# Buffer pools first in SBUF, x on a second queue, one output store, and a last weight load cut into 104 and 24 rows

## Chip, cores and metric

The kernel runs on one core of one Trainium2 chip. The metric is the device time of the program in microseconds (us), and lower is better. A run is one execution; the executions of one kernel lie within a few tenths of a per cent of each other. Now and then a run is far slower than the others of its kernel. Such runs are left out of every comparison here; there was one, a run of e9 with 240.59 us, whose granted clock was 1.0 as in the others, and it is marked.

## The reference

One decode step for four sequences: attention over a window of cached keys and values, and beside it an MLP block, all added to the input.

```python
# B=4, D=576, 32 query heads, 16 key/value heads of 128; F=4608; bf16
W = 2048                                    # the last 2048 positions of the cache
xn = layernorm(x)
q  = xn @ wq                                # [4, 32, 128]
p  = softmax(q @ k[:, :, -W:].T * 128**-0.5)
A  = (p @ v[:, :, -W:]) @ wo
# B: xn plus gelu(layernorm(xn) @ w1) shifted by rows and @ w2, then gelu(layernorm(.) @ w3) @ w4
# with one position per sequence every shift leaves zeros, so w1 and w2 drop out
out = x + A + xn + gelu(layernorm(xn) @ w3) @ w4
```

Every byte of wq, the K and V windows, wo, w3 and w4 is used once: the profile counts 87.17 MB read from HBM. There is little arithmetic per byte.

## The kernel before

The kernel is written around the stream of loads. They all go through the queue that SyncE issues, in the order in which they are needed: x, wq, then K and V of the sixteen heads with wo and w3 between them, and w4 at the end. Each K or V load brings 128 rows of 16,384 bytes, one row to a partition. Seven buffers hold K and V; wq, w3 and w4 use one buffer in turn.

```python
const = tile_pool("const", bufs=1)      # SBUF pools, in the order in which they get addresses
small = tile_pool("small", bufs=2)
kvp   = tile_pool("kv", bufs=7)
ktp   = tile_pool("kt", bufs=3)
ptp   = tile_pool("pt", bufs=3)
wp    = tile_pool("w", bufs=1)
wop   = tile_pool("wo", bufs=2)

x_bf = const.tile([B, D], BF16)
nc.sync.dma_start(out=x_bf[:], in_=x2)
wq_main = A_wq[0:KJ * P, :].rearrange("(p j) n -> p j n", j=KJ)
for j in range(KJ):                                            # four loads with 8 KB rows
    nc.sync.dma_start(out=wq_sb[:, j * NQ:(j + 1) * NQ], in_=wq_main[:, j, :])
# [... the rest of wq ...]

def load_kv(kind, h):
    t = kvp.tile([P, NC, Dh], BF16, tag="kv")                  # 128 x 16,384 bytes
    nc.sync.dma_start(out=t[:].rearrange("p c d -> p (c d)"),
                      in_=win[:, h].rearrange("b (p c) d -> p b (c d)", c=NC))

W4_PIECES = [0, 9, 18, 27, 32, 36]                             # five pieces of w4, in blocks of 1,152 bytes a row
def load_w4():
    for lo, hi in zip(W4_PIECES, W4_PIECES[1:]):
        # [... src is the half of w4 that the piece lies in ...]
        nc.sync.dma_start(out=t[:, lo:hi, :], in_=src[:, lo - e * NFH:hi - e * NFH, :])

def acc_matmuls(lhsT, rhs):                                    # four rows in each quadrant of acc
    for i in range(NQD):
        nc.tensor.matmul(out=acc[i * QD:i * QD + B, :], lhsT=lhsT, rhs=rhs[:, i * CW:(i + 1) * CW], ...)

# [... attention and the first matmul of the MLP ...]
for lo, hi in pieces[2:]:                                      # the last pieces of w4, as they land
    mlp_out(lo, hi)
fin = const.tile([P, CW], out.dtype)
nc.vector.tensor_copy(out=fin[:], in_=acc[:])
for i in range(NQD):                                           # four stores of four rows
    eng = nc.sync if i % 2 == 0 else nc.scalar
    eng.dma_start(out=o2[:, i * CW:(i + 1) * CW], in_=fin[i * QD:i * QD + B, :])
```

## Time and profile before

| | before |
|---|---|
| time | 216.24 us, median of 2 runs (216.18 to 216.3) |
| span of the profiled run | 214.6 us |
| PE, DVE and ACT busy | 56%, 55%, 33% |
| a K or V packet of 16,384 bytes | 611 ns, the next one 607 ns later on the same engine |
| first packet of wq starts | 2.15 us |
| last piece of w4 lands, first and last of sixteen engines | 205.50 and 210.21 us |
| end of fin to end of the span | 3.30 us |

The packet times come from the packet records of the trace, the landings from its semaphore updates: a whole load has sixteen, which I read as one from each of the sixteen DMA engines when its share is done. All times are counted from the profile's zero. The recorded prediction and expectations count packets and landings from a moment 0.24 us earlier: their 2.39 and 210.45 are the profile's 2.15 and 210.21. A difference of two such times isn't touched, but where they measure from an instruction to a landing, the figure is 0.24 us too long.

The first view is the profile's page of the kernel before: the span, the busy time of each engine, and in 40 slices of the span the busy share of the sixteen DMA engines in tenths and the GB/s they moved; then two DMA queues with packets, MB and busy share.

```profile
span 214.6 us, 6449 instructions
PE 121.0 (56%) x2893; PEld 94.9 (44%) x2893; DVE 118.0 (55%) x223; ACT 70.1 (33%) x258; POOL 6.1 (3%) x14
...
DMA  5999999999999999999999999999999999999960
GB/s 207 429 437 434 428 429 425 425 425 437 426 429 423 437 431 419 439 425 434 431 428 425 428 428 430 422 434 431 429 418 428 437 419 425 437 427 422 419 262 12
...
q1 hardware_dynamic: 7080, 87.17, 95.7%
q8 instruction: 22, 0.36, 0.6%
```

No compute engine is busy for more than 56% of the span, and the DMA engines are at 90% or more in slices 2 to 38. The load stream bounds the kernel. Time can be lost or won only at its head, by its rate in the middle, or in the two slices at its end.

The end of the chain of waits of the kernel before says the same (columns: start, duration, what ran or was waited for).

```profile
182.78 27.43 DMA w_sb<-in_B_w_dram
210.21 0.04 issue
210.26 0.68 PE acc L247 x16
...
210.96 0.31 DVE fin L480
```

The last link is a wait for the load of w4; only 16 matmuls and one copy stand between it and the stores.

The timeline of the kernel before, at its two ends (start, duration, engine, line, operation, output and input, count; in brackets the idle time before and what ended it; "q" behind an engine's name is its issuing of DMAs):

```profile
0.73 0.36 SPq L87 DMA_DIRECT2D x_bf<-in_A_x_dram  x1
...
1.16 1.31 SPq L92 DMA_DIRECT2D wq_sb<-in_A_wq_dram  x3
...
207.14 0.73 PE L247 MATMUL acc<-w_sb,gT 128*4 128x144 bf16 x36 [1.17 <-DMA w_sb<-in_B_w_dram]
...
208.88 0.77 PE L247 MATMUL acc<-w_sb,gT 128*4 128x144 bf16 x20 [1.00 <-DMA w_sb<-in_B_w_dram]
...
210.26 0.65 PE L247 MATMUL acc<-w_sb,gT 128*4 128x144 bf16 x16 [0.61 <-DMA w_sb<-in_B_w_dram]
...
210.96 0.31 DVE L480 CAST fin<-acc 128x144 bf16<-128x144 f32 x1 [5.87 <-PE acc L247]
211.29 0.63 SPq L483 DMA_DIRECT2D out_dram<-fin  x2
211.30 0.92 ACTq L483 DMA_DIRECT2D out_dram<-fin  x2
```

At the head, x is issued before wq and holds it up by 0.43 us. At the end, PE waits for the third, fourth and fifth piece of w4 in turn.

The 22 packets of instruction fetch (q8, 16 KB and 935 ns each) fall on eight of the sixteen engines in turn, and each sets its engine back by more than 1 us. (The packet records name no engine; that the same eight serve in turn is read from the landings.) Before the first fetch, at 15.01 us, the sixteen landings of a load lie within 0.57 us; in the next load one comes 1.58 us after the first, and the fifteen others still lie within 0.58. In the last piece, with two or three fetches for each of the eight, six of the sixteen landings come within 0.26 us of the first, two after 1.05 and 1.82 (why these two are late isn't shown), three after 3.1 to 3.3, and five after 4.2 to 4.7.

### The profile page before, as it was taken

What the parts mean: (1) busy time and instruction counts of PE and PEld (TensorE: products, weight loads), DVE (VectorE), ACT (ScalarE), POOL (GpSimd) and SP (SyncE); (2) the same over time, 40 slices, a digit from 0 to 9 for tenths busy, and PEclk for the clock granted to TensorE, in tenths of its full rate; (3) what the DMA queues carried; (4) which work ended last, traced back from release to release, by engine and by line L of the source; (5) the groups of instructions that cost most, each with busy time, mean ns of one, the idle gap of its engine ahead of it and who ended that gap; (6) DMA issues with size and microseconds to landing.
All of it is one profiled execution on the core that took longest, in us unless ns stands there. A gap on an engine that the chain in (4) does not pass through costs nothing. (4 is left out here: it accounts for less than half of the span.)

```text
span 214.6 us, 6449 instructions
## 1 busy us (share of the span) xinstructions
PE 121.0 (56%) x2893; PEld 94.9 (44%) x2893; DVE 118.0 (55%) x223; ACT 70.1 (33%) x258; POOL 6.1 (3%) x14
## 2 busy tenths in 40 slices
PE   0461355647470017157999577677474705779752
PEld 0350143445360015145899456555453604557641
DVE  5608799766470047348610798785573924854210
ACT  0000005571634001607070045570725340709600
POOL 5400100000000000000000000000000000000000
PEclk9999999999999999999999999999999999999995
DMA  5999999999999999999999999999999999999960
GB/s 207 429 437 434 428 429 425 425 425 437 426 429 423 437 431 419 439 425 434 431 428 425 428 428 430 422 434 431 429 418 428 437 419 425 437 427 422 419 262 12
DMA packets 7123, 87.58 MB, mean 408 GB/s; under 512 B 820, under 2 KB 824, under 8 KB 1336
## 3 DMA queue, kind: packets, MB, share of 16 engines
q1 hardware_dynamic: 7080, 87.17, 95.7%
q8 instruction: 22, 0.36, 0.6%
q14 instruction: 5, 0.04, 0.0%
q10 hardware_dynamic: 16, 0.00, 0.0%
HBM read 87.17 MB, written 0.00 MB: 406 GB/s over the span
## 5 line engine op out<-in xcount | busy, mean ns | idle before, releaser
L302 ACT ACTIVATE pt<-S 32x128 bf16<-32x128 f32 x256 | 68.5, 268 | 92.0 <-issue 55.3
L259 DVE STREAM_TRANSPOSE kt<-kn 128x1024 int32<-128x1024 int32 x64 | 74.3, 1205 | 11.4 <-DMA kn<-in_A_k_cache_dram 11.4
L313 PE MATMUL O<-pt,vn 128*128 128x8 bf16 x1024 | 37.4, 169 | 43.2 <-DMA vn<-in_A_v_cache_dram 41.7
L313 PEld LDWEIGHTS <-vn 128*128 128x128 bf16 x1024 | 34.4, 105 | 51.3 <-DMA vn<-in_A_v_cache_dram 43.6
L273 PE MATMUL S<-qz,kt 128*128 128x32 bf16 x1024 | 39.1, 189 | 25.2 <-DVE kt L259 25.2
L273 PEld LDWEIGHTS <-kt 128*128 128x128 bf16 x1024 | 33.6, 106 | 36.1 <-DVE kt L259 30.4
L287 DVE TENSOR_REDUCE m<-mxT 8x1 f32<-8x128 f32 x16 | 4.4, 277 | 42.6 <-PE mxT L285 42.6
L316 PE MATMUL O<-pt,ones_bf 128*128 128x64 bf16 x128 | 17.1, 226 | 0.0
L302 ACT ACT_TABLE_LOAD x1 | 1.3, 1283 | 32.6 <-DVE mx L280 32.6
L368 PEld LDWEIGHTS <-w_sb 128*128 128x128 bf16 x144 | 11.4, 164 | 0.5 <-issue 0.4
L368 PE MATMUL AB<-ln2T,w_sb 128*128 128x4 bf16 x144 | 11.5, 202 | 0.0
L280 DVE TENSOR_REDUCE mx<-S 128x8 f32<-128x512 f32 x16 | 10.4, 652 | 1.0 <-PE S L273 1.0
L295 PE MATMUL S<-dg,ones_bf 8*128 8x512 bf16 x16 | 9.6, 601 | 0.1
L265 PE MATMUL S<-negbig,ohT 4*128 4x512 bf16 x16 | 9.6, 601 | 0.0
L316 PEld LDWEIGHTS <-ones_bf 128*128 128x128 bf16 x128 | 8.4, 104 | 0.0
L370 PE MATMUL AB<-ln2T,w_sb 128*128 128x4 bf16 x36 | 7.3, 202 | 0.0
L247 PE MATMUL acc<-w_sb,gT 128*4 128x144 bf16 x144 | 4.8, 294 | 2.8 <-DMA w_sb<-in_B_w_dram 2.8
L324 DVE TENSOR_REDUCE dn<-O 128x8 f32<-128x64 f32 x16 | 3.3, 208 | 5.5 <-PE O L316 5.5
L375 DVE COPY g_x<-AB 128x144 f32<-128x144 f32 x1 | 0.3, 307 | 10.7 <-PE AB L370 10.7
L285 PE MATMUL mxT<-ident_f,mx 128*8 128x128 f32 x16 | 6.0, 374 | 0.3 <-DVE mx L280 0.3
L370 PEld LDWEIGHTS <-w_sb 128*128 128x128 bf16 x36 | 5.9, 165 | 0.0
L247 PEld LDWEIGHTS <-gT 128*4 128x4 bf16 x144 | 3.4, 104 | 3.6 <-issue 3.5
(72 smaller groups left out, 64.9 us busy)
## 6 DMA issues: line engine op xcount, KB each, us to landing
kn<-in_A_k_cache_dram SPq DMA_DIRECT2D x16, 2048.0 KB, 29.3
vn<-in_A_v_cache_dram SPq DMA_DIRECT2D x16, 2048.0 KB, 27.0
wo_sb<-in_A_wo_dram SPq DMA_DIRECT2D x4, 1152.0 KB, 28.8
w_sb<-in_B_w_dram SPq DMA_DIRECT2D x2, 2304.0 KB, 31.8
wq_sb<-in_A_wq_dram SPq DMA_DIRECT2D x4, 1024.0 KB, 4.9
w_sb<-in_B_w_dram SPq DMA_DIRECT2D x3, 1296.0 KB, 32.8
w_sb<-in_B_w_dram SPq DMA_DIRECT2D x2, 576.0 KB, 32.2
w_sb<-in_B_w_dram SPq DMA_DIRECT2D x1, 720.0 KB
```

The lines of the kernel that those rows point to most:

```text
L247: nc.tensor.matmul(out=acc[i * QD:i * QD + B, :], lhsT=lhsT, rhs=rhs[:, i * CW:(i + 1) * CW], start=False, stop=False, skip_group_check=True)
L259: nc.vector.transpose(out=kt[:], in_=src)
L265: nc.tensor.matmul(out=S_ps[h][:].rearrange("p g k j -> p (g k) j"), lhsT=ohT[:], rhs=nb, start=True, stop=False, skip_group_check=True)
L273: nc.tensor.matmul(out=S_ps[h][:, s * (SC // NQD) + g].rearrange("p k j -> p (k j)"), lhsT=kt[:, ib, g * NQD:(g + 1) * NQD, e:2 * QD:2].re ...
L280: nc.vector.reduce_max(out=mx[:], in_=S_ps[h][:].rearrange("p g k j -> p j (g k)"), axis=AX.X)
L285: nc.tensor.transpose(out=mxT[:], in_=st[h][:], identity=ident_f[:])
L295: nc.tensor.matmul(out=S_ps[h][:].rearrange("p g k j -> p (g k) j"), lhsT=ones_bf[0:NJ, :], rhs=dg, start=False, stop=False, skip_group_ch ...
L302: nc.scalar.activation(out=PT[h][kb * QD:(kb + 1) * QD, :, c4, :], in_=S_ps[h][c4 * QD:(c4 + 1) * QD, :, kb, :], func=ACT.Exp, scale=scale)
L313: nc.tensor.matmul(out=O_ps[h][:, 0:NJ], lhsT=vn[:, g * NQD + s, :], rhs=pt[:, g, s, :], start=(g == 0 and s == 0), stop=False, skip_group ...
L316: nc.tensor.matmul(out=O_ps[h][:, NJ:].rearrange("p (c j) -> p c j", j=NJ), lhsT=ones_bf[:], rhs=pt[:, g:g + DG, s, :], start=False, stop= ...
L368: nc.tensor.matmul(out=g_ps[:, i, :], lhsT=w3[:, j * F + e * (F // 2) + f0:j * F + (e + 1) * (F // 2):NFH], rhs=ln2T[:, j, :], start=False ...
L370: nc.tensor.matmul(out=g_ps[:, i, :], lhsT=w3[:, KJ * F + f0:KJ * F + F // 2:NFH], rhs=ln2T[:, KJ + e, :], start=False, stop=False, skip_g ...
```

## The change

The intent: start the stream earlier (x from ScalarE's queue, wq in fewer and longer rows), relieve some of the engines at the end (the last piece of w4 as 104 rows and 24 rows), and store once instead of four times. For the single store all 128 rows of acc are written by matmuls with 32 columns, most of them zero. The pools of the load buffers now come first in SBUF. The sum of x and xn (xsum) takes the buffer of xn_f. The helper that transposes K only moves within the file.

```diff
-    const = ctx.enter_context(tc.tile_pool(name="const", bufs=1))
-    small = ctx.enter_context(tc.tile_pool(name="small", bufs=2))
     kvp = ctx.enter_context(tc.tile_pool(name="kv", bufs=NKV))
-    ktp, ptp, wp, wop                      [in this order]
+    wp, wop, ktp, ptp, const, small        [in this order]
 [...]
-    nc.sync.dma_start(out=x_bf[:], in_=x2)
-    wq_main = A_wq[0:KJ * P, :].rearrange("(p j) n -> p j n", j=KJ)
-    for j in range(KJ):
-        nc.sync.dma_start(out=wq_sb[:, j * NQ:(j + 1) * NQ], in_=wq_main[:, j, :])
+    nc.scalar.dma_start(out=x_bf[:], in_=x2)
+    wq_main = A_wq[0:KJ * P, :].rearrange("(p j) n -> p (j n)", j=KJ)
+    for e in range(2):
+        lo, hi = e * 2 * NQ, (e + 1) * 2 * NQ
+        nc.sync.dma_start(out=wq_sb[:, lo:hi], in_=wq_main[:, lo:hi])
 [...]
-            nc.sync.dma_start(out=t[:, lo:hi, :], in_=src[:, lo - e * NFH:hi - e * NFH, :])
+            for p0, p1 in ((0, P),) if hi < NF else ((0, 104), (104, P)):
+                nc.sync.dma_start(out=t[p0:p1, lo:hi, :], in_=src[p0:p1, lo - e * NFH:hi - e * NFH, :])
 [...]
-    gT = const.tile([P, NF, B], BF16)
+    gT = const.tile([P, NF, QD], BF16)     [op likewise, and idz for the first matmuls into acc]
+    nc.gpsimd.memset(gT[:], 0.0)
 [...]
-            nc.tensor.matmul(out=acc[i * QD:i * QD + B, :], lhsT=lhsT, rhs=rhs[:, i * CW:(i + 1) * CW],
+            nc.tensor.matmul(out=acc[i * QD:(i + 1) * QD, :], lhsT=lhsT, rhs=rhs[:, i * CW:(i + 1) * CW],
 [...]
-    for i in range(NQD):
-        eng = nc.sync if i % 2 == 0 else nc.scalar
-        eng.dma_start(out=o2[:, i * CW:(i + 1) * CW], in_=fin[i * QD:i * QD + B, :])
+    nc.sync.dma_start(out=o2.rearrange("b (i n) -> i b n", i=NQD), in_=fin[0:P:RS, :])
```

One effect isn't in the diff: in the built kernels the K and V buffers, and those of w, wo, kt and pt, start at multiples of 256 bytes within a partition before the change (the first K buffer at byte 38,144), and 128 bytes past one after it (at byte 16,512), because what stands ahead of them is now four small constants, 128 bytes in all, no longer the pools const and small.

More of the change, by code (lines that the diff above doesn't have):

```diff
@@ L71 @@
     ctx.enter_context(tc.manual_schedule())
+    kvp = ctx.enter_context(tc.tile_pool(name="kv", bufs=NKV))
+    wp = ctx.enter_context(tc.tile_pool(name="w", bufs=1))
+    wop = ctx.enter_context(tc.tile_pool(name="wo", bufs=2))
+    ktp = ctx.enter_context(tc.tile_pool(name="kt", bufs=3))
+    ptp = ctx.enter_context(tc.tile_pool(name="pt", bufs=3))
     const = ctx.enter_context(tc.tile_pool(name="const", bufs=1))
     small = ctx.enter_context(tc.tile_pool(name="small", bufs=2))
-    kvp = ctx.enter_context(tc.tile_pool(name="kv", bufs=NKV))
-    ktp = ctx.enter_context(tc.tile_pool(name="kt", bufs=3))
-    ptp = ctx.enter_context(tc.tile_pool(name="pt", bufs=3))
-    wp = ctx.enter_context(tc.tile_pool(name="w", bufs=1))
-    wop = ctx.enter_context(tc.tile_pool(name="wo", bufs=2))
     ps_s = ctx.enter_context(tc.tile_pool(name="ps_s", bufs=3, space=PSUM))
@@ L83 @@
     ps_acc = ctx.enter_context(tc.tile_pool(name="ps_acc", bufs=1, space=PSUM))
-    x_bf = const.tile([B, D], BF16)
-    nc.sync.dma_start(out=x_bf[:], in_=x2)
-    wq_main = A_wq[0:KJ * P, :].rearrange("(p j) n -> p j n", j=KJ)
-    wq_sb = wp.tile([P, KJ * NQ + NQ // 2], BF16, tag="w", name="wq_sb")
-    for j in range(KJ):
-        nc.sync.dma_start(out=wq_sb[:, j * NQ:(j + 1) * NQ], in_=wq_main[:, j, :])
-    nc.sync.dma_start(out=wq_sb[:, KJ * NQ:], in_=A_wq[KJ * P:D, :].rearrange("r (e f) -> (r e) f", e=2))
     w_tiles = {}
@@ L109, in load_kv @@
         kv_tiles[kind, h] = t
+    x_bf = const.tile([B, D], BF16)
+    nc.scalar.dma_start(out=x_bf[:], in_=x2)
+    wq_sb = wp.tile([P, KJ * NQ + NQ // 2], BF16, tag="w", name="wq_sb")
+    wq_main = A_wq[0:KJ * P, :].rearrange("(p j) n -> p (j n)", j=KJ)
+    for e in range(2):
+        lo, hi = e * 2 * NQ, (e + 1) * 2 * NQ
+        nc.sync.dma_start(out=wq_sb[:, lo:hi], in_=wq_main[:, lo:hi])
+    nc.sync.dma_start(out=wq_sb[:, KJ * NQ:], in_=A_wq[KJ * P:D, :].rearrange("r (e f) -> (r e) f", e=2))
     def load_wo(p):
@@ L142 @@
     nc.gpsimd.memset(neg_half[:], -0.5)
+    RS = QD // B
     AB = ps_acc.tile([P, 512], F32)
@@ L184, with k_transpose @@
     xnT = transposed(xn_bf, "xnT")
+    kts = {}
+    def k_transpose(h, s):
+        src = kv_tiles["K", h][:].bitcast(I32)[:, s * SC:(s + 1) * SC, :].rearrange("p c (ib i) -> p ib c i", i=QD)
+        kt = ktp.tile([P, 2, SC, QD], I32, tag="kt")
+        nc.vector.transpose(out=kt[:], in_=src)
+        kts[h, s] = kt
     for j in range(KJ):
@@ L232 @@
     nc.vector.reduce_sum(out=own[:], in_=ident_f[:].rearrange("p (h d) -> p h d", h=WOH), axis=AX.X)
-    xsum = const.tile([B, D], F32)
+    idz = const.tile([B, QD], F32)
+    nc.gpsimd.memset(idz[:], 0.0)
+    nc.gpsimd.tensor_copy(out=idz[:, 0:QD:RS], in_=ident_f[0:B, 0:B])
+    xsum = xn_f
     nc.vector.tensor_tensor(out=xsum[:], in0=xn_f[:], in1=x_bf[:], op=ALU.add)
     for i in range(NQD):
-        nc.tensor.matmul(out=acc[i * QD:i * QD + B, :], lhsT=ident_f[0:B, 0:B], rhs=xsum[:, i * CW:(i + 1) * CW],
+        nc.tensor.matmul(out=acc[i * QD:(i + 1) * QD, :], lhsT=idz[:], rhs=xsum[:, i * CW:(i + 1) * CW],
                          start=False, stop=False, skip_group_check=True)
@@ L241 @@
     ln2T = transposed(ln2_bf, "ln2T")
-    gT = const.tile([P, NF, B], BF16)
+    gT = const.tile([P, NF, QD], BF16)
+    nc.gpsimd.memset(gT[:], 0.0)
+    op = const.tile([P, WOR, QD], BF16)
+    nc.gpsimd.memset(op[:], 0.0)
     def acc_matmuls(lhsT, rhs):
         for i in range(NQD):
-            nc.tensor.matmul(out=acc[i * QD:i * QD + B, :], lhsT=lhsT, rhs=rhs[:, i * CW:(i + 1) * CW],
+            nc.tensor.matmul(out=acc[i * QD:(i + 1) * QD, :], lhsT=lhsT, rhs=rhs[:, i * CW:(i + 1) * CW],
                              start=False, stop=False, skip_group_check=True)
-    kts = {}
     S_ps = {}
@@ L254 @@
     st = {}
-    def k_transpose(h, s):
-        src = kv_tiles["K", h][:].bitcast(I32)[:, s * SC:(s + 1) * SC, :].rearrange("p c (ib i) -> p ib c i", i=QD)
-        kt = ktp.tile([P, 2, SC, QD], I32, tag="kt")
-        nc.vector.transpose(out=kt[:], in_=src)
-        kts[h, s] = kt
     def k_mask(h):
@@ L350, in o_pick @@
                                 in1=own[:].unsqueeze(1).unsqueeze(3).to_broadcast([P, WOR, WOH, B]), op=ALU.mult)
-        op = small.tile([P, WOR, B], BF16, tag="op")
         with nc.allow_low_precision("one term is not zero"):
-            nc.vector.reduce_sum(out=op[:], in_=mk[:].rearrange("p i h b -> p i b h"), axis=AX.X)
-        st["op"] = op
+            nc.vector.reduce_sum(out=op[:, :, 0:QD:RS], in_=mk[:].rearrange("p i h b -> p i b h"), axis=AX.X)
     def o_proj(h):
@@ L358, in o_proj @@
             return
-        op = st.pop("op")
         for i in range(WOR):
@@ L381, in mlp_act @@
         nc.vector.tensor_scalar(out=u[:], in0=u[:], scalar1=0.5, scalar2=0.5, op0=ALU.mult, op1=ALU.add)
-        nc.vector.tensor_tensor(out=gT[:], in0=u[:], in1=xs[:], op=ALU.mult)
+        nc.vector.tensor_tensor(out=gT[:, :, 0:QD:RS], in0=u[:], in1=xs[:], op=ALU.mult)
     def mlp_out(lo, hi):
```

## The prediction

> **What bounds it.** The stream of loads. In the page's 40 slices the sixteen DMA engines are at 9 tenths or more in slices 2 to 38, mean 428 GB/s. In the packet records a 16,384-byte packet takes 611 ns and the next starts 607 ns after it, for 16 engines 432 GB/s: the middle (198 us) has 1% of slack. PE is busy 56%, DVE 55%. The chain of waits ends in 27 us of DMA into w_sb, 16 acc matmuls (0.68 us), fin (0.31 us), and 3.3 us from fin to the end. So three places can give time:
>
> 1. Head. Slice 1 moves 207 GB/s. SyncE issues x at 0.73 us, the first wq load at 1.16; the first wq packet starts at 2.39.
> 2. Skew at the end. The last w4 piece's sixteen completions (one per DMA engine, in the trace's semaphore updates) come between 205.74 and 210.45 us, mean 208.0: perfect balance would save 2.45 us. The skew grows at each 16 KB instruction fetch (queue 8, 22 packets, one engine each, eight engines in turn): six engines finish by 206.0, five between 210.0 and 210.5.
> 3. Stores. Two behind each other on each of two queues: first issue 211.29, last landing 213.33; the first SyncE store lands at 212.69.
>
> **What the change does.**
>
> - x on ScalarE's queue: the first wq issue moves from 1.16 to about 0.73, and the stream with it: -0.4 us. [...]here that time heads the bounding stream. wq in two loads with 16 KB rows: fewer packet overheads, -0.1 us.
> - Pools first: the load buffers move to addresses 128 modulo 256 (before: 0). The w4 pieces that start 128 bytes off, in source and target, take the same 389 ns per packet as aligned ones, so I expect nothing.
> - 104 + 24 rows. [...]The trace before has no such transfer. [...]But five engines are within 0.5 us of the last[...]. Between -0.5 and +0.4, centre -0.1.
> - acc matmuls with 32 instead of 4 columns: weight loads take about 31 ns in a row at 128 columns, 26 at 4. The last 16 stay near 0.65 us: 0 to +0.1.
> - One store: the last landing moves from 213.33 to about 212.8, not issued behind another: -0.5 us.
> - Extra memsets on idle GpSimd: nothing.
>
> **Sum.** 216.24 - 0.5 - 0.1 - 0.5 + 0.05 = 215.2 us; range 213.8 to 216.4. Over 2% faster would need 4.3 us; the three places hold about 3.5. Faster 0.03, same 0.95, slower 0.02.
>
> **What would show it.** First wq packet at about 2.0 us; the same 607 ns pitch; the last acc wait ending 0.5 us earlier; completions of the piece before the last still spread over 4 to 5 us; 2.8 instead of 3.3 us from fin to the end.
>
> **What would make it wrong.** [...]packets slowed by the 128-byte offset (5 ns of 607 would be +1.6 us); instruction fetches falling on other engines.

Passages are cut from the prediction, and below from some expectations, and marked. The sum came to 215.2 us: -0.5 for the head and wq, -0.1 for the 104 + 24 rows, -0.5 for the store, +0.05 for the matmuls. The -0.1 and its range of -0.5 to +0.4 stand as the author's estimate. Two other terms rest on the trace before. In it, wq packets of 8,192 bytes follow each other every 306 ns, and half of the 607 ns of a 16,384-byte packet is 303.5: over 32 such packets an engine (512 in all) that is 0.08 us, an estimate from these figures. And 16 weight loads of 128 columns take 0.50 us there, 31 ns each, and 36 of 4 columns 0.94 us, 26 ns each.

## More of the kernel before

The windows of the kernel before (stretch, its length, busy time and count of PE, PEld, DVE, ACT and POOL, granted clock, mean busy share of the DMA engines, GB/s):

```profile
60.00:100.00 40.00, 14.96 (x373) 11.51 (x371) 17.25 (x27) 11.20 (x42) 0.00 (x0) 1.00 1.01 428
...
200.00:204.00 4.00, 3.12 (x92) 2.56 (x89) 0.59 (x3) 1.83 (x7) 0.00 (x0) 1.00 0.99 415
204.00:208.00 4.00, 2.71 (x111) 2.15 (x108) 0.85 (x2) 0.00 (x0) 0.00 (x0) 1.00 0.69 289
```

Read the last two columns together. From 200 to 204 us the engines are busy throughout and move 415 GB/s. From 204 to 208 us they are busy for 0.69 of the time and move 289 GB/s, which is 419 GB/s for each unit of busy time: the engines that still work do so at full rate, and the others have finished.

## The result

The kernel after the change took 219.87 us (median of 2 runs, 219.64 to 220.09) against 216.24 us. The ratio is 1.0163, with a 95% interval of 1.0143 to 1.0184; the two runs of each kernel give 1.0168. In the experiments a ratio is the mean time of one kernel's fast runs over the mean time of the other's fast runs of the same rounds, so it isn't quite the ratio of the medians. The change cost 1.6%: within the class "within 2%", but outside the predicted range of 213.8 to 216.4 us and on the wrong side of the time before.

The page of the kernel after:

```profile
span 217.9 us, 6450 instructions
...
DMA  6999999999999999999999999999999999999940
GB/s 241 430 433 424 433 418 426 424 430 421 441 423 410 430 430 421 427 427 427 430 421 427 419 430 421 427 427 421 426 430 419 428 424 427 430 420 414 350 162 7
```

Slice 1 moves more than before (241 against 207 GB/s): the head gained. In slice 38 the engines are still 90% busy or more, as before, but move 350 instead of 419 GB/s, and in slice 39 they're 40% busy with 162 GB/s where they were 60% busy with 262.

The end of the chain of waits of the kernel after:

```profile
189.09 24.35 DMA w_sb<-in_B_w_dram
213.44 0.04 issue
213.48 0.69 PE acc L264 x13
...
214.20 0.31 DVE fin L487
```

It has the same shape: the load of w4, the last matmuls, fin. The matmuls with 32 columns take 0.69 us where those with 4 took 0.68. What moved is the end of the load: 213.44 instead of 210.21 us.

The timeline of the kernel after, at the same places:

```profile
0.73 0.89 SPq L109 DMA_DIRECT2D wq_sb<-in_A_wq_dram  x2
0.73 0.55 ACTq L104 DMA_DIRECT2D x_bf<-in_A_x_dram  x1
...
209.92 1.27 PE L264 MATMUL acc<-w_sb,gT 128*32 128x144 bf16 x36 [1.65 <-DMA w_sb<-in_B_w_dram]
...
211.80 0.79 PE L264 MATMUL acc<-w_sb,gT 128*32 128x144 bf16 x20 [0.61 <-DMA w_sb<-in_B_w_dram]
...
213.48 0.67 PE L264 MATMUL acc<-w_sb,gT 128*32 128x144 bf16 x16 [0.90 <-DMA w_sb<-in_B_w_dram]
...
214.20 0.31 DVE L487 CAST fin<-acc 128x144 bf16<-128x144 f32 x1 [7.86 <-PE acc L264]
214.54 0.67 SPq L488 DMA_DIRECT2D out_dram<-fin  x1
```

The third piece of w4, which is a whole load of 128 rows and stands ahead of the cut one, is already 2.78 us later than before (209.92 against 207.14). The windows of the kernel after:

```profile
60.00:100.00 40.00, 14.57 (x360) 11.12 (x356) 16.77 (x27) 10.79 (x41) 0.00 (x0) 1.00 1.00 425
...
200.00:204.00 4.00, 2.80 (x78) 2.34 (x79) 0.37 (x3) 2.99 (x12) 0.00 (x0) 1.00 1.01 426
204.00:208.00 4.00, 3.61 (x112) 3.03 (x105) 1.37 (x5) 0.00 (x0) 0.00 (x0) 1.00 0.91 257
```

Two things differ. In the middle, the same busy share moves 425 instead of 428 GB/s. From 204 to 208 us the engines are busier than before, 0.91 against 0.69, and yet move less, 257 against 289 GB/s. That is 282 GB/s for each unit of busy time where it was 419. Engines that are busy and move fewer bytes may be in each other's way; the experiments test that.

Laid end to end, the two traces give this account (the landings are last semaphore updates of a load):

| stretch | before | after | difference |
|---|---|---|---|
| to the first packet of wq | 2.15 | 1.76 | -0.39 |
| from there to the landing of the second piece of w4 (203.94; 205.04) | 201.79 | 203.28 | +1.49 |
| from there to the last landing of w4 (210.21; 213.44) | 6.27 | 8.40 | +2.13 |
| from there to the end of fin | 1.06 | 1.07 | +0.01 |
| from the end of fin to the end of the span | 3.30 | 3.36 | +0.06 |
| sum | | | +3.30, from 214.6 to 217.9 |

So there are two losses, one spread over the stream and one at its end.

The packet records show the first. Of the 16,384-byte packets that start after about 8 us, 0.5% are 1 to 19 ns slower than the usual 611 ns before the change, and 62.8% after it. Here is one engine's packets between 72 and 84 us (ns, in order; a dot is a packet of another size), which before the change are all 611 in the same stretch:

```
after: 619 612 615 614 . 618 611 612 619 612 615 615 619 .
```

The same records show the second: packets of 10,368 bytes, which take 389 ns in the kernel before (854 ns for the two that meet an instruction fetch), take up to 779 ns from 205 us on even where they meet no fetch, and 4,608-byte packets take 322 ns at their ninth decile where they took 178.

### The profile page after: what moved, and what is told of

It is laid out like the page before. It is cut to its first block, busy times and chain, and to the rows that moved or that the text cites. A ratio compares the mean times of both kernels' runs of the same rounds, so it can differ in the third digit from the quotient of the medians.

```text
span 217.9 us, 6450 instructions
## 1 busy us (share of the span) xinstructions
PE 121.9 (56%) x2893; PEld 96.0 (44%) x2893; DVE 119.2 (55%) x223; ACT 70.1 (32%) x258; POOL 8.1 (4%) x18
## 5 line engine op out<-in xcount | busy, mean ns | idle before, releaser
L264 PE MATMUL acc<-w_sb,gT 128*32 128x144 bf16 x144 | 5.6, 322 | 3.6 <-DMA w_sb<-in_B_w_dram 3.2
L264 PEld LDWEIGHTS <-gT 128*32 128x32 bf16 x144 | 4.1, 136 | 4.7 <-issue 3.9
```

The source lines that it names most:

```text
L264: nc.tensor.matmul(out=acc[i * QD:(i + 1) * QD, :], lhsT=lhsT, rhs=rhs[:, i * CW:(i + 1) * CW], start=False, stop=False, skip_group_check= ...
```

## The experiments

My theory had two parts. First: the load buffers' start, 128 past a multiple of 256, slows packets in the whole stream. Second: the cut of the last load by rows lets early engines, which have nothing else left, write rows that slow the late engines. By what mechanism rows could do so no run here shows, and the theory of the rows is that it matters which rows are written at the same time. The rivals were these: that the cut merely hands more packets to late engines, at full rate; that a second load at the end costs in itself; that the extra time in the middle comes from other pool order, other queues or instruction fetches; and that the new matmuls or the single store cost what they were meant to save.

All ratios are to the kernel before in the same rounds, whose medians lay between 216.15 and 216.36 us; square brackets are 95% intervals.

### Undo one loss at a time: e1, e2, e3

e1 takes the changed kernel and loads the last piece whole.

```diff
-            for p0, p1 in ((0, P),) if hi < NF else ((0, 104), (104, P)):
-                nc.sync.dma_start(out=t[p0:p1, lo:hi, :], in_=src[p0:p1, lo - e * NFH:hi - e * NFH, :])
+            nc.sync.dma_start(out=t[:, lo:hi, :], in_=src[:, lo - e * NFH:hi - e * NFH, :])
```

> The changed kernel, but with the last piece of w4 as one load of 128 rows. In the changed kernel's trace the load before the last three ends 1.1 us later than before (205.28 against 204.18), the last one 3.2 us later (213.68 against 210.45): 2.1 us come in the last 8 us, in which the 389 ns packets of w4 take up to 775 ns. Theory[...]: 217.8 us, all 4,608-byte packets of w4 back at 178 ns, spread of the last completions about 5 us. Rival (only the two rows more on late engines cost): 219.5 us or more, as these are worth 0.35 us.

e2 takes the changed kernel and puts 128 bytes ahead of the load buffers, so that they start at multiples of 256 again.

```diff
+    padp = ctx.enter_context(tc.tile_pool(name="pad", bufs=1))
+    pad = padp.tile([P, 64], BF16)
+    nc.gpsimd.memset(pad[:], 0.0)
     kvp = ctx.enter_context(tc.tile_pool(name="kv", bufs=NKV))
```

> The changed kernel with a pad tile of 128 bytes ahead of the load pools, so that all load buffers start at 0 modulo 256 instead of 128; the split stays. Theory (the 128-byte offset slows the packets: mean 618.8 against 613.3 ns for 16,384 bytes): packets back to 611 ns without the 612 to 624 of the changed kernel, the stream 1.5 us shorter, 218.4 us. Rival (order of pools, or the phase in which the engines start after the new wq loads, makes it): packets stay spread over 611 to 624, 219.9 us.

e3 does both.

> The changed kernel with both: aligned by the pad of 128 bytes, and the last piece in one load. Theory (the two causes are separate and add): 219.9 - 2.1 - 1.5 = 216.2 us or a little less, since the head is 0.4 us earlier: 215.8 to 216.3. If a third cause is at work (32-column acc matmuls, the single store), it stays above 216.5.

| | offset | last load | time | ratio to before |
|---|---|---|---|---|
| after | 128 | cut | 219.87 | 1.0163 [1.0143, 1.0184] |
| e1 | 128 | whole | 217.02 | 1.0032 [1.0018, 1.0045] |
| e2 | 0 | cut | 218.39 | 1.0097 [1.0083, 1.0111] |
| e3 | 0 | whole | 215.37 | 0.9958 [0.9945, 0.9970] |

The 618.8 ns in e2's expectation include the packets of wq, which are of this size only after the change and slow while the stream starts; without them the mean is 616.5 ns.

The two losses are separate and add up: the offset costs 1.65 us with the whole load (217.02 - 215.37) and 1.48 with the cut one (219.87 - 218.39); the cut costs 2.85 us with the offset and 3.02 without. The rest of the change gains 0.9 us (0.42% of 216.2), so e3 beats both kernels. Both e1 and e3 came out about 0.8 us below their expectations (217.8 and 216.2), because not all of the cut's cost lies in its packets. In the profiled spans, after is 2.67 us longer than e1: 2.20 us of it by the landing of w4, 0.48 behind fin. e2 is 3.26 us longer than e3: 2.54 by the landing, 0.24 in the last 16 matmuls, 0.48 behind fin. The 0.48 us come back in e6 and e11 below. The share of slow packets goes with the offset alone: 63.1% in e1, 0.3% in e2, 0.4% in e3.

The windows of e2, and then of e3, around the end of the stream:

```profile
204.00:208.00 4.00, 2.22 (x68) 2.01 (x68) 0.85 (x2) 0.00 (x0) 0.00 (x0) 1.00 0.77 198
```

```profile
204.00:208.00 4.00, 2.81 (x106) 2.18 (x105) 0.85 (x2) 0.00 (x0) 0.00 (x0) 1.00 0.65 268
```

In the four microseconds before, the two are alike (416 and 418 GB/s). Here e3's engines are busy for 0.65 and move 268 GB/s (412 for each unit), while e2's are busy for 0.77 and move 198 (257). The loss of the cut lies here.

The timelines of e2, and then of e3, show on whom it falls:

```profile
208.91 1.27 PE L267 MATMUL acc<-w_sb,gT 128*32 128x144 bf16 x36 [2.69 <-DMA w_sb<-in_B_w_dram]
...
210.85 0.79 PE L267 MATMUL acc<-w_sb,gT 128*32 128x144 bf16 x20 [0.68 <-DMA w_sb<-in_B_w_dram]
...
212.46 0.67 PE L267 MATMUL acc<-w_sb,gT 128*32 128x144 bf16 x16 [0.81 <-DMA w_sb<-in_B_w_dram]
```

```profile
206.81 0.75 PE L266 MATMUL acc<-w_sb,gT 128*32 128x144 bf16 x36 [0.40 <-DMA w_sb<-in_B_w_dram]
...
208.55 0.50 PE L266 MATMUL acc<-w_sb,gT 128*32 128x144 bf16 x20 [0.99 <-DMA w_sb<-in_B_w_dram]
...
209.92 0.43 PE L266 MATMUL acc<-w_sb,gT 128*32 128x144 bf16 x16 [0.87 <-DMA w_sb<-in_B_w_dram]
```

Of the 2.54 us by which the last matmuls start later in e2, 2.10 are there at the third piece (208.91 against 206.81). That piece is loaded whole in both kernels and stands two loads ahead of the cut one. The late engines were still busy with it when the early ones, up to 4.9 us ahead at the second piece, had begun on the cut load.

### Other cuts of the last load: e5, e6

Both start from e2, the aligned kernel. e5 cuts at row 64. The pages count 776 packets under 512 bytes in e3, 785 in e2 and 792 in e5. That fits one for each semaphore update, with sixteen in the whole load of e3, 13 and 12 in the two loads of e2, and sixteen in each of e5's. So I take it (an estimate) that every engine has as many rows in e5 as in the whole load, and that nothing is handed from one engine to another.

```diff
-            for p0, p1 in ((0, P),) if hi < NF else ((0, 104), (104, P)):
+            for p0, p1 in ((0, P),) if hi < NF else ((0, 64), (64, P)):
```

> The aligned changed kernel (that of e2 and e3) with the last piece in two loads of 64 rows instead of 104 and 24.[...] Theory[...]: as bad as 104 + 24 or worse, 217.5 to 219 us, with 4,608-byte packets of 350 ns, twice the 178, and slow packets of the pieces before it. Rivals (the cost of 104 + 24 is the two rows more on late engines, or fewer than 16 engines in a load): 215.4 us, as e3.

e6 also makes two loads of the last piece, but cuts it by columns, with all 128 rows in both.

```diff
+            for i0, i1 in ((lo, hi),) if hi < NF else ((lo, lo + 2), (lo + 2, hi)):
+                nc.sync.dma_start(out=t[:, i0:i1, :], in_=src[:, i0 - e * NFH:i1 - e * NFH, :])
```

> The aligned changed kernel with the last piece in two loads of all 128 rows, half of the columns each (2,304-byte rows). Control for the number of loads: if two loads at the end instead of one were the cost, it is as slow as e2 (218.4 us). Theory[...]: 215.4 to 215.6 us[...].

e5 took 218.42 us, 1.0098 [1.0082, 1.0114], the same as the 104-row cut of e2. e6 took 215.86 us, 0.9976 [0.9964, 0.9989], 0.5 us over e3. Here are the windows of e5, and then of e6:

```profile
204.00:208.00 4.00, 2.26 (x72) 1.98 (x69) 0.85 (x2) 0.00 (x0) 0.00 (x0) 1.00 0.72 203
```

```profile
204.00:208.00 4.00, 3.41 (x104) 2.68 (x97) 0.82 (x2) 0.00 (x0) 0.00 (x0) 1.00 0.65 266
```

e5 moves 282 GB/s for each unit of busy time, e6 moves 409. In e5's packet records the leading engines need some 275 to 365 ns for 4,608 bytes, about twice the 178 ns of the whole load, and 10,368-byte packets of the late engines take up to 779 ns without meeting an instruction fetch. In e6 no packet is stretched (93 ns for 2,304 bytes throughout), and its last landing, 209.91 us, is that of e3, 209.87. So a second load isn't the cause, nor, if e5's engines share the rows evenly, an uneven share of packets; loads of rows other than the full 128 are. Why these slow the packets isn't shown. The half microsecond of e6 over e3, by which it also misses its expectation, is at the very end (3.34 us from fin to the end of the span against 2.87), not in the loads. e5, which has it too, is 2.6 us slower than e6, and that is about what the rows cost by themselves.

### Adjacent rows and rows four apart, by themselves: e10, e13, e9

To test the choice of rows without the skew at the end, I put eight loads of eight rows each (9,216 bytes a row, data of wo into a buffer that nobody reads) behind wq in e3. In e10 the eight rows of a load lie four apart; in e13 they're adjacent. Bytes and packets are the same. That eight engines carry such a load, one row each, was my estimate: e10's 64 packets of 347 ns between 13.38 and 16.51 us make 7.1 at a time in the mean.

```diff
+    dummy = wop.tile([P, WOR, D], BF16, tag="wo", name="dummy")
+    for g in range(8):
+        # e10:  rows = dummy[32 * (g // 4) + g % 4:32 * (g // 4) + 32:4]
+        # e13:  rows = dummy[8 * g:8 * g + 8]
+        nc.sync.dma_start(out=rows.rearrange("p i n -> p (i n)"), in_=wo_src[0][8 * g:8 * g + 8])
```

> As e9, [...]load g writes eight partitions four apart (0, 4, ..., 28, and so on)[...]. Theory[...]: 347 ns per packet, as in the loads of wo; 215.4 us + 0.3 us for 0.6 MB more[...]. Rival: packets as slow as in e9.

> The kernel of e3 with eight extra loads of 8 rows (9,216 bytes each, never read) right behind wq. Load g writes partitions 8g to 8g + 7[...]. Theory[...]: the packets of 9,216 bytes of these loads take up to four times the 347 ns, 1,000 to 1,400 ns. Rival (a load on fewer than 16 engines, or its reading side, is slow): the same packet times as in e10.

The profile of e9 fell on its slow run (240.59 us), so I ran the same kernel once more as e13.

> The kernel of e9 again, because its profiled execution fell in the slow state (240.59 us; its other runs 221.2 to 222.5). Theory[...]: in a fast execution the packets of 9,216 bytes of the eight extra loads take about 700 ns again, twice the 347 of e10, and the time is about 221.7 us. Rival (the slow packets of e9 belong to its slow state): 347 ns.

The windows of e10, and then of e13, over these loads:

```profile
13.60:15.00 1.40, 1.40 (x59) 1.40 (x57) 0.00 (x0) 0.00 (x0) 0.00 (x0) 1.00 0.58 225
15.00:16.60 1.60, 0.68 (x25) 0.59 (x23) 0.83 (x5) 0.00 (x0) 0.00 (x0) 1.00 0.75 246
```

```profile
13.60:15.00 1.40, 1.40 (x58) 1.40 (x56) 0.00 (x0) 0.00 (x0) 0.00 (x0) 1.00 0.68 130
15.00:16.60 1.60, 0.68 (x22) 0.59 (x19) 0.83 (x5) 0.00 (x0) 0.00 (x0) 1.00 0.50 81
```

In e10 all 64 packets take exactly 347 ns, as a 9,216-byte packet does in the whole stream, and they run from 13.38 to 16.51 us. In e13 the first eight take 347 ns, and then they rise to about 900 (median 886), done at 20.34 us. The windows have 130 and 81 GB/s where e10 has 225 and 246. The times agree: e10 218.57 us, 1.0112 [1.0098, 1.0125]; e13 221.83 us, 1.0261 [1.0236, 1.0287]; the three fast runs of e9 221.24 to 222.46 us (median 221.58), 1.0260 [1.0235, 1.0286]. Adjacent rows cost 3.3 us. They differ from spread rows in the rows written, and in the time to issue a load, which is shorter for them (0.29 against 0.62 us) and so can't be the cost. So it is shown that which rows are written stretches packets; by what mechanism isn't shown. The size was missed as well: e9's expectation said 1,000 to 1,400 ns and e13's 700, and it was 886, in e9's own profile 690. (e10 itself is slower than e3, and than the 215.7 us of its expectation. If eight engines carry eight packets more each, that is 8 x 347 ns or 2.8 us, an estimate; its last landing is 3.2 us later.)

### The offset alone, on the kernel before: e4, e7, e14, e12

These four take the kernel before and put a small tile ahead of all pools. Nothing else changes: the order of pools, the queues, the stores and the whole loads stay.

```diff
+    padp = ctx.enter_context(tc.tile_pool(name="pad", bufs=1))
+    pad = padp.tile([P, 64], BF16)     # e4: 128 bytes; e7: 16, 32 bytes; e14: 32, 64 bytes; e12: 128, 256 bytes
+    nc.gpsimd.memset(pad[:], 0.0)
     const = ctx.enter_context(tc.tile_pool(name="const", bufs=1))
```

> The kernel before with nothing but a pad tile of 128 bytes ahead of its pools: its load buffers move from 0 to 128 modulo 256. Theory of the offset: 16,384-byte packets at a mean of about 618 ns (before 613), 612 to 624 in the mode where before had 611, and 216.2 + 1.5 = 217.7 us. Rival (no cost of the offset): 216.2 us and 611 ns throughout.

> The kernel before with a pad of 32 bytes: load buffers at 32 modulo 256. If any offset between source and target modulo 256 costs, the stream is longer by about what 128 bytes cost (217.8 us) or more[...]; if only 128 is bad, 216.3 us.

> The kernel before with a pad of 64 bytes: load buffers at 64 modulo 256. If every offset modulo 256 costs, 217.7 us or more (128 bytes: 217.8, 32 bytes: 218.5) and packets of 16,384 bytes at a mean of 617 ns or more; if only 32 and 128 are bad, 216.2 us.

> Control for e4 and e7: the kernel before with a pad of 256 bytes, all addresses moved but load buffers at 0 modulo 256 again. Theory (only the offset modulo 256 counts): 216.3 us and 611 ns throughout. If any moving of the buffers costs (or the pad's memset), 217.5 us or more.

| | shift | time | ratio | slow 16 KB packets | mean packet |
|---|---|---|---|---|---|
| before | 0 | 216.24 | 1 | 0.5% | 613.3 ns |
| e7 | 32 | 218.47 | 1.0096 [1.0081, 1.0112] | 99.3% | 618.0 |
| e14 | 64 | 217.88 | 1.0076 [1.0064, 1.0089] | 92.6% | 617.2 |
| e4 | 128 | 217.78 | 1.0066 [1.0053, 1.0078] | 67.3% | 616.6 |
| e12 | 256 | 216.33 | 1.0011 [0.9998, 1.0025] | 0.5% | 613.4 |

The windows of e4, and then of e12, in the middle of the stream:

```profile
60.00:100.00 40.00, 15.22 (x378) 11.72 (x373) 16.74 (x27) 10.46 (x39) 0.00 (x0) 1.00 1.01 425
```

```profile
60.00:100.00 40.00, 15.11 (x377) 11.67 (x379) 17.40 (x27) 11.42 (x43) 0.00 (x0) 1.00 1.01 429
```

A shift by 256 bytes costs nothing that the interval can tell, so neither the pad nor its memset does. A shift by less than 256 costs 1.4 to 2.1 us (0.66% to 0.96% of 216.2). This is the start modulo 256, on a kernel with none of the other parts of the change. Slow packets explain most of it: added up for one engine in e4 they make about 1.0 us. The instruction fetches, which fall on the late engines, take 1,064 instead of 935 ns each, and three of them make 0.39 us. Together that is 1.4 us, against 1.5 measured.

### Which buffers have to be off: e15, e16, e17, e18

Is a packet slow because of its own target address? e15 puts the 128 bytes between pt and w, so that only w and wo are off.

```diff
     ptp = ctx.enter_context(tc.tile_pool(name="pt", bufs=3))
+    padp = ctx.enter_context(tc.tile_pool(name="pad", bufs=1))
+    pad = padp.tile([P, 64], BF16)
+    nc.gpsimd.memset(pad[:], 0.0)
     wp = ctx.enter_context(tc.tile_pool(name="w", bufs=1))
```

> The kernel before with a pad of 128 bytes between the kv, kt and pt pools and the pools of w and wo: only the targets of wq, w3, w4 and wo are at 128 modulo 256. Theory (a packet is slow by its own offset): the 16,384-byte packets of k and v stay at 611 ns, those of wo, w3 and w4 get slower by up to 8 ns, and the time is about 0.3 us more, 216.5 us (a quarter of the bytes, 1.5 us for all). Rival (some load with an offset disturbs all others): packets of k and v at 612 to 624 as in e4, and 217.5 us.

e16, e17 and e18 make each K and V buffer 256 bytes longer and choose where the data starts: at 0 for both (e16), at 128 bytes for K alone (e17), at 128 bytes for V alone (e18). To make room, xsum shares the buffer of xn_f in all three, as it does in the changed kernel.

```diff
-        t = kvp.tile([P, NC, Dh], BF16, tag="kv")
+        t = kvp.tile([P, NC * Dh + 128], BF16, tag="kv")
+        off = 64 if kind == "K" else 0          # e17; e16: 0 and 0; e18: 0 if K else 64
+        flat = t[:, off:off + NC * Dh]
```

> Control: the kernel before with each k and v buffer 256 bytes longer than its data (xsum put into xn_f to make room), data at 0 modulo 256. Both theories: 216.2 us, packets at 611 ns.

> As e16, but the data of k alone lie 128 bytes into their buffers, v at 0. Theory (a packet is slowed by its own offset[...]): only packets of k are at 612 to 624, those of v at 611, and the time is 0.2 to 0.75 us more, 216.4 to 217.0 us. Rival (engines that read data at an offset disturb the DMA engines' writes): packets of v, wo and w3 are slower too.

> As e17 with k and v exchanged: v at 128, k at 0. Theory: only packets of v are at 612 to 624, 216.4 to 217.0 us. Rival: packets of k, wo and w3 too.

| | off by 128 | time | ratio | slow 16 KB packets |
|---|---|---|---|---|
| e15 | w, wo | 216.38 | 1.0009 [0.9995, 1.0023] | 0.6% |
| e16 | none | 216.14 | 0.9997 [0.9985, 1.0010] | 0.5% |
| e17 | K | 216.47 | 1.0011 [0.9997, 1.0025] | 2.4% |
| e18 | V | 216.42 | 1.0010 [0.9997, 1.0022] | 3.0% |

None of the parts costs anything that its interval can tell from zero, and the centres of e15, e17 and e18 add up to 0.30%, or 0.65 us, of e4's 1.4. So my theory in its simple form, that a packet is slow because its own target is off, fell: K and V are most of the stream, and moving one or the other made 2 to 3% of the packets slow, not half of them. Its rival, that reads of offset data by the compute engines disturb the stream, isn't seen either: PE and DVE read the offset K or V in e17 and e18. What stays open is why nearly all buffers have to be off before it costs. Differences remain untested: kt and pt, which the compute engines write and read, are off in e4 and in the changed kernel, and aligned in e15, e17 and e18, and in e4 the tiles of const and small have moved too. I have no run with kt and pt off alone, nor one with K and V off together.

### The head and the stores: e8, e11

e8 is the kernel before with the new head only: x on ScalarE's queue, wq in two loads.

```diff
-    nc.sync.dma_start(out=x_bf[:], in_=x2)
+    nc.scalar.dma_start(out=x_bf[:], in_=x2)
 [... wq in two loads, as in the change ...]
```

> The kernel before with x on ScalarE's queue and wq in two loads of 16 KB rows, nothing else. Theory: the first wq packet starts at 1.98 us instead of 2.39, and all landings come 0.4 us earlier: 215.85 us. Rival (the head is hidden later by waits for buffers): 216.3 us with the last landing at 210.4.

It took 216.05 us, 0.9985 [0.9971, 0.9999]: a gain of about 0.3 us, with the first packet at 1.77 instead of 2.15 us. The step was right.

e11 is e3 with four stores on two queues again, each of four rows that lie eight apart.

```diff
-    nc.sync.dma_start(out=o2.rearrange("b (i n) -> i b n", i=NQD), in_=fin[0:P:RS, :])
+    for i in range(NQD):
+        eng = nc.sync if i % 2 == 0 else nc.scalar
+        eng.dma_start(out=o2[:, i * CW:(i + 1) * CW], in_=fin[i * QD:(i + 1) * QD:RS, :])
```

> The kernel of e3 with the four small stores of before (two on each queue) instead of the single one. In e3 the single store takes 0.70 us to issue and lands 2.04 us after fin's end; in the kernel before two stores take 0.63 us and the last lands 2.06 us after fin's end. Theory: the single store gains nothing, 215.4 us. The prediction's view (0.5 us gained): 215.9 us.

The end of the timeline of e11:

```profile
210.68 1.48 SPq L492 DMA_DIRECT2D out_dram<-fin  x2
210.68 1.33 ACTq L492 DMA_DIRECT2D out_dram<-fin  x2
```

It took 217.00 us, 1.0041 [1.0029, 1.0054], 1.6 us more than e3 and more than either forecast. But it doesn't undo the change cleanly: with rows eight apart a store takes 0.60 to 0.76 us to issue, while three of the four stores of the kernel before, whose rows are adjacent, take about 0.3. Two such stores on SyncE take 1.48 us here and 0.63 before. So e11 shows that four stores of spread rows are bad, not what one store saves over the old four. That comes from the traces: from the end of fin to the last landing it's 1.80 us with one store and 1.83 with the old four. From the end of fin to the end of the span it's 3.30 us before and 3.36 after, but 2.88 and 2.87 in e1 and e3. The difference between the last two figures and the others goes with an idle stretch of SyncE of about 0.45 us at the very end: between two drains in after, e2, e5, e6, e8 and e11, between two semaphore instructions in before, and absent in e1, e3, e10 and e13. It isn't the number of loads, since e10 and e13 have eight more than e3; why it appears isn't shown. So what the single store saves by itself stays open.

## Why the prediction was wrong, and where it was right

What held. The stream of loads bounds both kernels, and only the head, its rate and its end moved the time. The head gave 0.39 us in the trace (-0.4 predicted) and about 0.3 us in e8. The matmuls with 32 columns cost 0.69 us for the last 16 against 0.68. (In e3 the 16 take 0.46 us. The columns aren't the reason, since the kernels with 4 columns show the same two values, 0.68 in before and e15 and 0.45 in e4 and e17; nor is the granted clock, at 1.00 in both after and e3. I leave it open. It puts 0.23 us of chance into any comparison of two single profiles.) The memsets cost nothing that shows. Without the two losses the rest of the change takes 215.37 us, e3, where the sum said 215.2.

What failed, in the order of size:

1. "104 + 24 rows. ... Between -0.5 and +0.4, centre -0.1." Measured: +2.13 us at the end of the trace, +2.85 and +3.02 us in the timed pairs, of which 0.48 are the idle stretch at the end that goes with the cut. The numbers of engines that I had assumed were right: the trace has 13 semaphore updates for the 104-row load and 12 for the 24-row load. Which engines they are it doesn't show. The step that failed is that I charged each packet 174 ns, the pitch of the 4,608-byte packets in the trace before, whatever rows the other engines write. In whole loads the packets keep their usual time (178 ns for 4,608 bytes at the ninth decile in before, 93 ns for 2,304 bytes throughout in e6). Beside a load of 104, 24 or 64 rows they don't: 4,608 bytes take 322 ns at the ninth decile in after, and some 275 to 365 ns on the leading engines of e5. With engines up to 4.7 us apart, the early ones were in the cut load while the late ones still worked on the third piece, and these were slowed where they could least afford it. The risk that the narrower transfers run slowly stood under what would make the prediction wrong, without a size and without moving the range.
2. "Pools first: ... so I expect nothing." Measured: +1.49 us in the trace, +1.48 and +1.65 us in the timed pairs, 1.4 us in e4 with nothing else changed. The evidence was real: the w4 pieces 128 bytes off take 389 ns in the stream before. But they are off in source and target alike, and the change shifts targets alone; and they are single loads in a stream otherwise aligned. e15, e17 and e18 show that targets off alone, for some of the loads, cost next to nothing, while nearly all off cost 1.5 us. The inference from one load to all of them was the failing step. The size in the list of risks ("5 ns of 607 would be +1.6 us") was right partly by luck: in e4 the packets of 16,384 bytes rose by 3.3 ns in the mean, all packets of an engine together by about 1.0 us, and slower instruction fetches made most of the rest.
3. "One store: ... -0.5 us." Measured: +0.06 us in the profile of after, about -0.4 in e1 and e3, which lack the idle stretch at the end. The landing was mis-sized: I had it about 1.3 us after fin, since no other store is issued ahead of it, and it comes 1.80 us after fin in after and in e3 alike, no earlier than the last of the old four (1.83). The single store alone takes 0.67 us to issue, as long as SyncE's old two together (0.63).

Taken together: -0.39 + 1.49 + 2.13 + 0.01 + 0.06 is +3.30 us in the profiled spans, where the prediction had -1.05.

Left open: why an offset below 256 bytes costs only when nearly all buffers have it; how rows are dealt to the engines for 104, 24 and 64 rows, which I inferred only from packets that stretch; why packets stretch to 886 ns with adjacent rows, where they take 347 with rows four apart; and the idle 0.45 us at the end.

## What to carry to other kernels

In a kernel bound by its loads, if you cut a last load at all, cut it by columns and keep all 128 rows: here loads of some of the rows slowed engines that were still busy with earlier loads, and cost 2.5 to 2.6 us more than a cut by columns. After reordering pools, look at where the load buffers start modulo 256, and pad if they have moved off; here 128 bytes were worth 1.5 us. When a risk in your own list has a size larger than the gain you predict, build it into the range, or find a transfer in the trace that settles it.
